# A gated state-space and attention mix: rotation tables grown from a base made on GpSimd, value sums dealt per period, the last exps cut by rows

## The chip, the cores and the metric

One core of one Trainium2 chip. The metric is the device time of one execution in microseconds (us). The kernel before took 921.59 us (median of 3 runs, 921.59 to 921.75). Below, "the span" is the time of the profiled execution from its first to its last instruction; it is 1.7 to 1.8 us shorter than the device time. PE is TensorE (PEld its weight loads), ACT is ScalarE, DVE is VectorE, POOL is GpSimd, SP is SyncE.

## The reference, cut to what matters

One sequence of 2048 positions with 1024 channels; the output is a gated mix of a diagonal state-space model and of 32-head attention.

```python
def reference(A_x, A_Lambda_re, ..., B_wqkv, B_wo, gate_w):
    x = A_x
    g = _sigmoid((x * gate_w).sum(-1, keepdims=True))
    # A: 1024 complex states
    Lam_bar = jnp.exp(dt * Lam)
    for t in range(L):
        h = Lam_bar[None, :] * h + Bu[:, t, :]        # Bu = x @ B_bar^T
    y = 2.0 * einsum("blp,dp->bld", hseq, Cmat).real + x * Dskip
    # B: 32 heads of 32 channels, no mask
    p = _softmax(scores * (Dh ** -0.5))                # [32, 2048, 2048]
    b = (p @ v) @ wo
    return g * a + (1 - g) * b
```

The softmax needs 32 x 2048 x 2048 exponentials, and they are most of the work of ScalarE.

## The kernel before

The attention runs as 512 "bursts" (the kernel's periods). Each makes scores for 4 heads, 256 queries and 256 keys in PSUM, takes two exps of 128x1024 from them and later multiplies the results with the values. In the bursts of a fixed list, half of the first exp is made on VectorE, in four instructions:

```python
def exp(self, B, z, s):
    ...
    if z == 0 and B in DVB:                 # DVB: the list of shared bursts, 96 of 512
        self.dve_exp(B, s, p)
    else:
        self.act(lambda e: e.activation(self.tile[p], ps[:, 2 * s:2 * s + 2, :], ACT.Exp, ...), ...)

def dve_exp(self, B, s, p):
    ...
    self.S.op("act", ...)                   # a half exp, 128x512, on ScalarE
    self.S.op("dve", ... tensor_scalar(xi, ps[:, 2 * s + 1, :], ...), name="exp_a")
    self.dx += [(0.603, ... "exp_b"), (0.603, ... "exp_c"), (0.603, ... "exp_d"), ...]
```

All other work fills the gaps: projections, the scan of the state-space part (by rotation tables `Et`, 512 steps for each block of 128 states), and the output projection. A small scheduler in Python puts each engine's instructions into a fixed order before the program is built; each engine then runs its own in that order.

The rotation tables are products of a fine and a coarse table, one block of states after the other:

```python
def table_ops(self, j):
    ...
    for k, y in ((0, lo), (2, lor)):
        ops.append((1.136, ... e.tensor_tensor(prod[:, k:k + 2], hi, y, ALU.mult) ...))
    for r, op in ((0, ALU.subtract), (1, ALU.add)):
        ops.append((0.6, ... e.tensor_tensor(out, prod[:, 2 * r], prod[:, 2 * r + 1], op) ...))
```

The end, after the last burst: value sums, normalization, transpose, output projection on top of preloaded sums, evacuation, two stores; and a check of the softmax's denominators whose flag every engine reads and branches on (the other path, a slower method, is never taken here):

```python
def tail(self):
    ...
    self.pv([(NBURST - 2, q) for q in range(4)])     # value sums of burst 510
    preload()
    self.pv([(NBURST - 1, q) for q in range(4)])     # value sums of burst 511
    dve(... reciprocal ...)
    for t in range(2):
        dve(... norm ...); S.op("pe", ... "xp")      # normalize, transpose
    ...                                              # check, projection, evacuation
    self.st_out(14 + r, fb)                          # two stores of 256 KB

def stream(name, e):
    S.emit(name, e, sems, MARK_AT[name], ...)        # a hint for the branch, some way ahead of it
    e.wait_ge(sems[fast.flag_op.lane], fast.flag_op.tick)
    e.reg_load(r, flag[0:1, 0:1])
    br = e.br_cmp(r, 0, on_true="done_" + name, on_false="bad_" + name, comp_op="IS_EQ")
```

## Time and profile before

| part of the profiled span | us | how read |
|---|---|---|
| start to the first exp | 9.82 | timeline of ScalarE |
| first exp to the end of the last exp | 901.70 | 9.82 to 911.52 |
| end of the last exp to the end of the last evacuation | 3.80 | to 915.32 |
| from there to the end of the span | 4.99 | to 920.31 |

The lines that carry the first two terms are in the prediction. Timeline of TensorE in the kernel before; columns: start, length, engine, line, operation, out<-in, count, and in brackets how long the engine was idle before and what released it:

```profile
909.26 1.17 PE L1765 MATMUL f_ps<-f_V,f_pt 128*128 128x33 bf16 x32
910.28 1.02 PE L2051 MATMUL f_ps<-f_Et,f_ident 128*128 128x512 bf16 x4
911.14 0.80 PE L1765 MATMUL f_ps<-f_V,f_pt 128*128 128x33 bf16 x16
912.64 0.50 PE L2066 MATMUL f_ps<-f_ident,f_On 128*128 128x128 bf16 x2 [0.70 <-DVE f_On L2063]
```

TensorE works on through the last exps: value sums of the burst before, the preload (four matmuls in 1.02 us), value sums of the last burst, and then one wait of 0.70 us for the normalization.

### The profile page before, as it was taken

How to read it: one execution, taken by the hardware profiler on the slowest of the kernel's cores; microseconds unless marked ns; L12 is line 12 of the kernel's file. 1: busy time of each engine (PE TensorE's matmuls, PEld its weight loads, DVE VectorE, ACT ScalarE, POOL GpSimd, SP SyncE). 2: the span in 40 equal slices, each digit the busy share in tenths (PEclk: the TensorE clock that was granted, in tenths of full speed). 3: DMA queues.
4: the chain of work that ended last, by engine and by line, in shares of the span. 5: the costliest groups of instructions: out<-in, count | busy, mean ns of one | idle time of the engine just before them, and what ended most of it. 6: DMA issues, size and time to landing. Idle time of an engine off the chain costs nothing.

```text
span 920.3 us, 33392 instructions
## 1 busy us (share of the span) xinstructions
PE 884.9 (96%) x14969; PEld 516.3 (56%) x15188; DVE 758.0 (82%) x1369; ACT 904.4 (98%) x1034; POOL 6.5 (1%) x31
## 2 busy tenths in 40 slices
PE   8999999999999999999999999999999999999996
PEld 4556655755575555565557555556655655555553
DVE  2799999999989889999889975669999866675665
ACT  6999999999999999999999999999999999999996
POOL 0000000000000000000000000000000000000000
PEclk9999999999999999999999999999999999999998
DMA  9546822213302324112142113123320212524312
GB/s 200 111 82 114 120 48 40 47 42 73 82 9 56 62 59 93 47 36 53 51 82 43 42 46 86 44 63 53 51 64 8 68 60 82 162 78 131 113 63 75
DMA packets 166436, 65.35 MB, mean 71 GB/s; under 512 B 146704, under 2 KB 154896, under 8 KB 166288
## 3 DMA queue, kind: packets, MB, share of 16 engines
q1 hardware_dynamic: 164128, 62.62, 30.6%
q8 instruction: 120, 1.97, 0.9%
q10 hardware_dynamic: 2160, 0.53, 0.3%
q14 instruction: 28, 0.23, 0.1%
HBM read 21.24 MB, written 12.58 MB: 37 GB/s over the span
## 4 chain that ended last, share of the span: by engine, by line
ACT 69%; PE 25%; DVE 2%; SPq 1%; issue 1%; DMA 1%; DVEq 0%
ACT f_pt L1693 59%; PE f_ps L1765 7%; PE f_ps L1677 5%; PE f_ps L1513 4%; PE f_ps L1485 4%; PE f_ps L1453 3%; ACT f_wb L1716 2%; ACT f_OT L1693 2%; ACT f_Et L1693 2%; ACT f_cT_re L1693 2%; ACT f_cT_im L1693 2%; PE f_ps L1473 1%; ACT f_ub L1716 1%; SPq L1080 1%; DMA f_xT<-in_A_x_dram 1%
## 5 line engine op out<-in xcount | busy, mean ns | idle before, releaser
L1693 ACT ACTIVATE f_pt<-f_ps 128x1024 bf16<-128x1024 f32 x848 | 801.8, 1141 | 1.2 <-PE f_ps L1677 1.0
L1765 PEld LDWEIGHTS f_ps<-f_V,f_pt 128*128 128x128 bf16 x6784 | 235.0, 96 | 136.5 <-issue 86.6
L1765 PE MATMUL f_ps<-f_V,f_pt 128*128 128x33 bf16 x6784 | 288.4, 178 | 0.3
L1677 PE MATMUL f_ps<-f_Q,f_K 32*128 32x256 bf16 x4096 | 217.9, 273 | 6.8 <-ACT f_cT_re L1693 1.0
L1677 PEld LDWEIGHTS f_ps<-f_Q,f_K 32*128 32x128 bf16 x4096 | 70.3, 92 | 122.6 <-ACT f_pt L1693 62.3
L1485 PE MATMUL f_ps<-f_xT,f_wb 128*128 128x512 bf16 x449 | 117.5, 377 | 7.2 <-issue 2.4
L1453 PE MATMUL f_ps<-f_xT,f_wb 128*128 128x512 bf16 x406 | 106.6, 378 | 5.0 <-issue 1.0
L1399 DVE TENSOR_TENSOR_SCAN f_ht<-f_pf,f_init,f_ut 128x512 bf16<-128x512 f32 x64 | 81.0, 1274 | 0.0
L1717 DVE TENSOR_SCALAR f_wb<-f_ps 128x512 f32<-128x512 f32 x77 | 52.8, 686 | 27.7 <-PE f_ps L1677 27.2
L1513 PE MATMUL f_ps<-f_cT_im,f_hp 128*128 128x512 bf16 x183 | 69.1, 378 | 3.0 <-DVE f_Ag L1522 0.5
L1540 PE MATMUL f_ps<-f_wb,f_OT 128*128 128x512 bf16 x219 | 58.0, 378 | 2.1 <-DVE f_xT L1546 0.2
L1473 PE MATMUL f_ps<-f_wb,f_xT 128*128 128x128 bf16 x896 | 59.1, 219 | 0.0
L1485 PEld LDWEIGHTS f_ps<-f_xT,f_wb 128*128 128x128 bf16 x512 | 40.2, 96 | 33.4 <-issue 1.2
L1513 PE MATMUL f_ps<-f_cT_re,f_hp 128*128 128x512 bf16 x153 | 57.8, 378 | 0.6
L1716 ACT ACTIVATE f_wb<-f_ps 128x512 bf16<-128x512 f32 x77 | 53.8, 699 | 0.0
L1724 DVE SCALAR_TENSOR_TENSOR f_wb<-f_Ag,f_wb 128x512 int16<-128x512 f32 x77 | 52.7, 684 | 0.7
L1723 DVE SCALAR_TENSOR_TENSOR f_Ag<-f_wb,f_Ag 128x512 f32<-128x512 uint16 x77 | 52.7, 685 | 0.6
L1722 DVE SCALAR_TENSOR_TENSOR f_Ag<-f_wb 128x512 f32<-128x512 uint16 x77 | 52.6, 683 | 0.1
L1453 PEld LDWEIGHTS f_ps<-f_xT,f_wb 128*128 128x128 bf16 x464 | 36.2, 96 | 28.7 <-issue 0.4
L1473 PEld LDWEIGHTS f_ps<-f_wb,f_xT 128*128 128x128 bf16 x896 | 50.5, 97 | 0.2
L1546 DVE SCALAR_TENSOR_TENSOR f_xT<-f_ps,f_gcol,f_hp 128x512 bf16<-128x512 f32 (+1 forms) x28 | 21.0, 751 | 26.6 <-PE f_ps L1540 26.6
L1391 DVE TENSOR_TENSOR f_tq<-f_ht,f_Et 128x1024 bf16<-128x1024 bf16 x64 | 42.5, 685 | 0.3
(143 smaller groups left out, 872.1 us busy)
## 6 DMA issues: line engine op xcount, KB each, us to landing
ag_scratch<-f_Ag SPq DMA_DIRECT2D x32, 256.0 KB, 2.0
f_hp<-ag_scratch SPq DMA_DIRECT2D x32, 256.0 KB, 2.8
f_wb<-in_B_wqkv_dram SPq DMA_DIRECT2D x21, 256.0 KB, 4.1
out_dram<-f_xT SPq DMA_DIRECT2D x16, 256.0 KB, 2.0
f_xa<-in_A_x_dram SPq DMA_DIRECT2D x32, 64.0 KB, 2.0
f_pf<-in_A_x_dram SPq DMA_DIRECT2D x32, 64.0 KB, 2.0
f_wb<-in_B_wo_dram SPq DMA_DIRECT2D x1, 1024.0 KB
f_OT<-f_On SPq DMA_TRANSPOSE x63, 2.3
```

The lines of the kernel that those rows point to most:

```text
L1399: ops.append((1.192, lambda ri=ri: dve(lambda e: e.tensor_tensor_scan(ht[:, ri, :], rr, ut[:, ri, :], self.init[:, ri, j:j + 1], ALU.mult, ...
L1453: mms.append((1, lambda e, f, l, a=a: e.matmul(ps[:, bank, :], w[:, g % 2, part, a, :], xT[:, a, 512 * ch:512 * (ch + 1)], start=f, stop=l ...
L1473: m = e.matmul(ps[:, bank, 128 * q:128 * (q + 1)], xT[:, a, 128 * kt:128 * (kt + 1)], w[:, g % 2, 2, a, :], start=(a == 0), stop=(a == 7))
L1485: mms.append((1, lambda e, f, l, a=a: e.matmul(ps[:, 7, :], bT[:, n % 2, ri, a, :], xT[:, a, 512 * ch:512 * (ch + 1)], start=f, stop=l), [ ...
L1513: mms.append((1, lambda e, f, l, j=j, ri=ri: e.matmul(ps[:, 7, :], hp(tq, ri, j), cT[ri][:, j, 512 * cb:512 * (cb + 1)], start=f, stop=l), ...
L1540: mms.append((1, lambda e, f, l, j=j: e.matmul(ps[:, 7, :], OT[:, j, 256 * qb + 128 * r:256 * qb + 128 * (r + 1)], wo[j][0][:, 512 * cb:51 ...
L1677: m = e.matmul(ps[:, 2 * sl[z] + h % 2, 256 * kl:256 * (kl + 1)], K[32 * h:32 * h + 32, g % 2, 128 * kt:128 * (kt + 1)], Q[32 * h:32 * h + ...
L1693: self.act(lambda e: e.activation(self.tile[p], ps[:, 2 * s:2 * s + 2, :], ACT.Exp, bias=OCTAVES * LN2, scale=LN2 / 128), [("S", s)], [("p ...
L1716: self.S.op("act", lambda e: e.activation(t[:, 0, :], ps[:, 2 * s, :], ACT.Exp, bias=OCTAVES * LN2, scale=LN2 / 128), reads=[("S", s)], wr ...
L1717: self.S.op("dve", lambda e: e.tensor_scalar(xi, ps[:, 2 * s + 1, :], BITS_0, BITS_MIN, ALU.add, ALU.max), reads=[("S", s)], writes=[("xi" ...
L1723: (0.603, lambda: self.dve(lambda e: e.scalar_tensor_tensor(xw, lo, CUBE_C, xw, ALU.add, ALU.mult), [I, W], [W], "exp_c")),
L1765: m = e.matmul(ps[:, 6, o:o + 33], self.tile[p][:, h2, 256 * kl + 128 * qt:256 * kl + 128 * (qt + 1)], V[:, g % 2, 2 * i + kl, h, :], star ...
```

## The change

Its intent: free VectorE from table work, so that more exps can be shared; fit TensorE's value sums to each period; shorten the end.

- The table's base of 128 steps is made once for all states by six operations on GpSimd; VectorE doubles it twice. The copies of the last scan column also go to GpSimd.
- The list of shared bursts grows from 96 to 101.
- The value sums are dealt per period from burst 72 on.
- The last burst's exps are cut by query halves, the tail works half by half, with four stores of 128 KB; the check moves behind the evacuations.
- GpSimd takes no part in the branch at the end.

The diff, cut to its core (`...` are cuts):

```diff
-DVB_RUNS = ((65, 65), ..., (489, 493), (498, 498), (501, 501), (508, 508))
+DVB_RUNS = ((65, 65), ..., (489, 493), (498, 498), (501, 501), (506, 510))
...
+        def products():
+            for n, (u, v) in enumerate(((0, 0), (1, 1), (0, 1), (1, 0))):
+                self.pool(lambda e, ...: e.tensor_tensor(pr[n], hi[u], lo[v], ALU.mult), ...)
+                if n % 2:
+                    self.pool(lambda e, ...: e.tensor_tensor(out, pr[n - 1], pr[n], ALU.add if r else ALU.subtract), ...)
+        ops.append((0.0, products))
...
     def table_ops(self, j):
-        for k, y in ((0, lo), (2, lor)):
-            ops.append((1.136, ... e.tensor_tensor(prod[:, k:k + 2], hi, y, ALU.mult), ...))
-        for r, op in ((0, ALU.subtract), (1, ALU.add)):
-            ops.append((0.6, ... e.tensor_tensor(out, prod[:, 2 * r], prod[:, 2 * r + 1], op), ...))
+        op(0.27, ... e.tensor_scalar(S[:, :, 0:128], bj[:, :, 0:128], w(1, 0), None, ALU.mult), ...)
+        for r, alu in ((0, ALU.subtract), (1, ALU.add)):
+            op(0.27, ... e.scalar_tensor_tensor(bj[:, r, 128:256], bj[:, r, 0:128], w(0, 0), S[:, 1 - r, 0:128], ALU.mult, alu), ...)
+        op(0.40, ... e.tensor_scalar(S, bj, w(1, 1), None, ALU.mult), ...)
+        op(0.34, ... e.tensor_copy(Et[:, :, j, 0:256], bj), ...)
+        for r, alu in ((0, ALU.subtract), (1, ALU.add)):
+            op(0.40, ... e.scalar_tensor_tensor(Et[:, r, j, 256:512], bj[:, r], w(0, 1), S[:, 1 - r], ALU.mult, alu), ...)
...
     def burst(self, B):
+        if B == NBURST - 1:                      # rows: both score buffers, 128 queries at a time
+            for t in range(2):
+                self.act(lambda e, t=t: e.activation(self.tile[...], rows[:, :, 128 * t:128 * (t + 1)], ACT.Exp, ...), ...)
+            return lambda: None
...
     def tail(self):
-        self.pv([(NBURST - 2, q) for q in range(4)])
+        self.pv([(last - 1, q) for q in range(4)])
         preload()
-        self.pv([(NBURST - 1, q) for q in range(4)])
-        dve(... reciprocal ...)
+        pv(0)
+        norm(0)
+        pv(1)
+        xp(0)
+        norm(1)
+        out(0)
+        xp(1)
+        out(1)
+        evac(0, 0, "dve")
+        evac(0, 1, "dve")
+        evac(1, 0, "act")
+        evac(1, 1, "dve")
+        for _, f in self.check(62, 64, 62, 65, 2):
+            f()
...
+            if name == "pool":
+                S.emit(name, e, sems)
+                return
             S.emit(name, e, sems, MARK_AT[name], ...)
-            if name == "pool":
-                for _ in range(272):
-                    e.nop()
```

## The prediction

> **What bounds the kernel now.** I read the page of the profile first (busy time, slices), then the chain of waits in order of time, then the timeline at both ends, then the groups of instructions by shape.
>
> The page:
>
> ```profile
> PE 884.9 (96%) x14969; PEld 516.3 (56%) x15188; DVE 758.0 (82%) x1369; ACT 904.4 (98%) x1034; POOL 6.5 (1%) x31
> ACT  6999999999999999999999999999999999999996
> ```
>
> ScalarE is full in every slice but the first and the last. PE looks nearly as full, but the groups show that its weight loads for the scores stood 62.3 us waiting for an exp to free a score buffer, so PE has room. The question is whether ScalarE's work is tight. The chain in order of time answers it:
>
> ```profile
> 145.05 19.25 ACT f_pt L1693 x21
> 164.79 54.08 ACT f_pt L1693 x59
> 904.61 0.49 ACT f_ub L1716
> ```
>
> The reader should divide: 54.08 / 59 = 0.9166 us is the pace of one full exp (128x1024), back to back; a half exp (128x512, the other half being made on VectorE) takes 0.49. The groups give the counts: 848 + 24 + 20 + 18 + 18 = 928 full and 77 + 19 = 96 half exps. At that pace they need 928 x 0.9166 + 96 x 0.49 = 850.6 + 47.0 = 897.6 us. The timeline shows when they ran (start, length):
>
> ```profile
> 9.82 1.94 ACT L1693 ACTIVATE f_pt<-f_ps 128x1024 bf16<-128x1024 f32 x2 [0.57 <-PE f_ps L1677]
> ...
> 904.97 6.55 ACT L1693 ACTIVATE f_pt<-f_ps 128x1024 bf16<-128x1024 f32 x7
> 910.93 0.47 PEld L1765 LDWEIGHTS f_ps<-f_V,f_pt 128*128 128x128 bf16 x8
> ...
> 914.05 1.27 DVE L2091 SCALAR_TENSOR_TENSOR f_xT<-f_ps,f_Et 128x512 bf16<-128x512 f32 x2
> 914.81 0.92 SPq L1571 DMA_DIRECT2D out_dram<-f_xT  x2
> ```
>
> From 9.82 to 911.52 are 901.7 us, so in 900 us ScalarE lost only about 4.1 us to waits. The span of 920.3 is therefore: 9.8 before the first exp, 897.6 of exps, 4.1 of waits, and 8.8 after the last exp (3.8 until the last evacuation ends at 915.32, the last store issued by 915.73, the rest its landing and the closing wait). Only those four terms can be changed.
>
> **What the Trainium skill says.** "ScalarE: Activation LUTs", section "What ACT_TABLE_LOAD costs", gives one element per cycle and lane at 1.2 GHz, 0.833 ns per element, for every function. The trace agrees: 0.9166 - 0.49 = 0.427 us for 512 elements, 0.833 ns each. A full exp can't get cheaper; only its work can be moved.
>
> "GPSIMD Engine Reference", section "3.1 Elementwise — side-by-side cycle accounting", gives 4497 ns for a two-input fp32 operation of 2048 elements. This trace has GpSimd only on tiny tiles (128x8 at 0.2 to 0.3 us), so it can't confirm it. My estimate from that figure: 2.25 us for 1024 elements.
>
> "SBUF — State Buffer", section "Who interferes with whom", says that a GpSimd operation that reads SBUF and a VectorE operation with two SBUF inputs, or in a 2-port mode, exclude each other for a whole instruction. No run here shows it yet; the changed kernel may.
>
> "VectorE: DVE Perf Modes", section "The perf-mode tier table (the rule you actually need)", says that each operation is capped at the mode it has a program for, single-source ones higher than two-source ones. The trace agrees:
>
> ```profile
> L1289 DVE SCALAR_TENSOR_TENSOR f_OT<-f_OT 128x400 f32<-128x400 f32 x1 | 0.6, 568 | 0.0
> L1290 DVE TENSOR_SCALAR f_OT<-f_OT 128x400 f32<-128x400 f32 x1 | 0.4, 369 | 0.0
> L1296 DVE TENSOR_SCALAR f_W<-f_W 128x16 f32<-128x16 f32 x1 | 0.2, 175 | 0.0
> L1294 DVE SCALAR_TENSOR_TENSOR f_W<-f_OT 128x16 f32<-128x16 f32 x1 | 0.2, 175 | 0.0
> ```
>
> With the 16-element forms this makes (369 - 175) / 384 = 0.51 ns per element for the one-input fp32 form and (568 - 175) / 384 = 1.02 ns for the two-input form, on 0.16 to 0.17 us fixed.
>
> **The change part by part.**
>
> (1) More half exps. The diff doesn't say so in words, but the list of bursts whose exp is shared grows from 96 to 101 (29 added, 24 removed; the count by groups of 64 bursts is +3 in the second, +1 in the seventh and eighth). ScalarE saves 5 x 0.427 = 2.1 us. VectorE gains 5 x 4 instructions of 0.685 (rows below) = 13.7 us.
>
> ```profile
> L1717 DVE TENSOR_SCALAR f_wb<-f_ps 128x512 f32<-128x512 f32 x77 | 52.8, 686 | 27.7 <-PE f_ps L1677 27.2
> L1370 DVE TENSOR_TENSOR f_OT<-f_OT 128x1024 f32<-128x1024 f32 x16 | 19.0, 1215 | 0.0
> L1374 DVE TENSOR_TENSOR f_Et<-f_OT 128x512 bf16<-128x512 f32 x16 | 11.0, 685 | 0.1
> ```
>
> (2) What pays for it on VectorE. The old rotation tables go: 16 x 1.215 + 16 x 0.685 = 30.4 us. The new ones cost per block of states one tensor_scalar of 256 (0.30), two two-input operations of 128 (2 x 0.29), a tensor_scalar of 512 and a copy of 512 (2 x 0.43), two two-input operations of 256 (2 x 0.42): 2.6 us, 20.6 for eight. The sine and cosine series shrinks from 400 to 224 columns: 15 two-input operations save 0.18 each and 7 one-input ones 0.09, together 3.3. The 24 copies of the last scan column (0.16 each, 3.8) go to GpSimd. Freed: 9.8 + 3.3 + 3.8 = 16.9, against 13.7 added, so VectorE ends near 755 us, no fuller than now. None of this is on the path by itself; it makes room for (1).
>
> (3) The base on GpSimd: four products and two sums of 1024 elements, by my estimate 6 x 2.25 = 13.5 us, where before it was busy 6.5 us in all. The order of instructions shows that the last input is made just after the seventh key evacuation, which in the trace of before ran at 25.2; so the base begins near 26.7 and ends near 40.3. The first VectorE instruction that waits for it follows the gate's reciprocal, at 40.1 to 40.5 in the trace of before. Between lie only evacuations from PSUM, which don't use the shared port. Eight table instructions (2.6 us) follow, and then the first evacuation of u, at 43.3 before. So the base is just in time; any delay beyond half a microsecond would push that evacuation, and PE with it.
>
> (4) Value sums dealt per period. A full period lasts 2 x 0.917 = 1.83 us on ScalarE and a shared one 1.41; PE's load per period is now matched to that instead of a fixed 5 or 3 quarters. This can only take from the 4.1 us of waits, of which about 0.9 lie in the opening and 1.0 before burst 72, where nothing is dealt anew. I take 0.9 of the remaining 2.2 as saved, a guess at under half, since the five new shared periods are themselves short ones that PE has to keep up with.
>
> (5) The end. The last two exps are cut by query halves, so the sums, the normalization and the transpose of the first half run under the last exp. Estimate from the last exp's end: sums 0.6, reciprocal and normalization 0.55, transpose and copy 0.6, projection 0.6, evacuation 0.7, with the first half's pieces queued in front on PE and VectorE: about 3.6 instead of 3.8. The final stores are four of 128 KB instead of two of 256, the first ones earlier, so the last has less data in front of it. The last landing took 4.1 us (915.7 to 919.8), while the median store took 2.0; I take 0.7 off. Sum for the end: 0.9. The check moves behind the evacuations; with 0.9 for its instructions and 1.0 for reading the flag (0.74 on SyncE before) it ends under the landing.
>
> (6) GpSimd out of the end branch: it was idle there and finished at 917.7, before the last store landed. Nothing. The three-fold matmuls of the rest are 8 more, at 1.02 / 4 = 0.26 at most, 2 us of PE in periods where PE waits. Nothing.
>
> Sum: 921.6 - 2.1 - 0.9 - 0.9 = 917.7 us.
>
> **The rivals.** First, the base comes late. For it: an untested GpSimd rate, the exact fit in (3), and VectorE issuing in order, so that evacuations queue behind the wait. If the six operations took twice the estimate, VectorE would stand 13 us and ScalarE perhaps 8 of them: 925 us or more. Against it: the placement looks deliberate, and the chain of before shows ScalarE not even losing 1 us there. I give a loss over 1 us one chance in six.
>
> Second, the room on VectorE isn't where it is needed. From 40 to 150 us it was busy 101.5 of 110 us, and from 150 to 300 141.1 of 150; three of the added shared exps fall just there. If evacuations came late, waits would grow by what the exps saved: 920 to 922 us. Against it: the freed table work lies in the same stretch.
>
> Third, a better end and a better fit: if the last landing took the usual 2 us, the end would give 2 instead of 0.9, and if the dealing removed 2 of the waits, the total would be 915.5. Much below that there is nothing: 9.8 + 895.5 of exps + 7 + 1.3 (measured time over span) is 913.6 with no wait at all.
>
> **Range and chances.** The sure part is 2.1; the two guesses are 0.9 each with an error near 1; the first rival lengthens the upper side. So 917.7, with 915.6 to 920.4 for eight in ten. Two per cent faster would be 903.2, which ScalarE's 895.5 us of exps alone exclude (9.8 and about 7 come on top). Two per cent slower is 940: only a broken schedule. Faster 0.01, same 0.98, slower 0.01.
>
> **What would show it.** 923 full and 101 half exps at 0.917 and 0.49; ScalarE's first exp to its last about 898.7 us; GpSimd near 25 us busy with six instructions near 2.2 us ending before 41; VectorE near 755; the last exp's end to the end of the span about 7.9 us. I am wrong if the full exp's pace changes, if VectorE waits for GpSimd over 1 us near 40, if waits inside the exps exceed 5 us, or if the end takes as long as before.

## More of the kernel before

The busy times in stretches; columns: stretch, its length, busy time (and count) of PE, PEld, DVE, ACT, POOL, then the granted clock of TensorE, the DMA share and GB/s:

```profile
909.00:912.00 3.00, 2.80 (x62) 1.92 (x57) 2.11 (x9) 2.52 (x3) 0.00 (x0) 1.00 0.19 72
```

The clock is at 1.00 here.

## The result and the profile after

The changed kernel took 925.45 us (median of 4 runs, 924.98 to 926.12), the kernel before 921.67 on the same chip. The ratio is 1.004, with a 95% interval of 1.0023 to 1.0058: the same within 2%, but slower by 3.8 us where 3.9 us less were forecast. (A ratio here is the mean time of one kernel's fast runs over the mean of the other's in the same rounds, so not quite the ratio of the medians.)

The same four terms of the span:

| part of the profiled span | before | after | forecast change | measured change |
|---|---|---|---|---|
| start to the first exp | 9.82 | 9.55 | 0 | -0.27 |
| first exp to the end of the last exp | 901.70 | 899.04 | -3.0 | -2.66 |
| last exp to the end of the last evacuation | 3.80 | 8.85 | -0.2 | +5.05 |
| last evacuation to the end of the span | 4.99 | 5.79 | -0.7 | +0.80 |
| span | 920.31 | 923.23 | -3.9 | +2.92 |

The second term came out nearly as forecast, and the end did not. (The first is no gain: in the fourteen traces the first exp starts at 9.55 to 10.16.) The page of the changed kernel:

```profile
PE 905.0 (98%) x15196; PEld 514.1 (56%) x15196; DVE 756.5 (82%) x1391; ACT 901.4 (98%) x1033; POOL 31.0 (3%) x63
PEclk9999999999999999999999999999999999999997
```

ScalarE has 3.0 us less to do (904.4 before), VectorE is no fuller than it was. (The trace of before lacks some 220 matmul records, so its lower PE figure is no change.) Was GpSimd in time with the base? Timeline of GpSimd, and the first instruction of VectorE that uses the base:

```profile
26.03 3.82 POOL L1319 TENSOR_TENSOR f_hp<-f_rc 128x1024 f32<-128x1024 f32 x2 [23.12 <-DVE f_rc L1310]
29.93 2.37 POOL L1323 TENSOR_TENSOR f_OT<-f_hp 128x1024 f32<-128x1024 f32 x1
32.24 3.83 POOL L1319 TENSOR_TENSOR f_hp<-f_rc 128x1024 f32<-128x1024 f32 x2
36.15 2.36 POOL L1323 TENSOR_TENSOR f_OT<-f_hp 128x1024 f32<-128x1024 f32 x1
```

```profile
39.92 0.35 DVE L1400 TENSOR_SCALAR f_Ag<-f_OT,f_rc 128x256 f32<-128x256 f32 x1
```

The base ends at 38.51; its first user starts at 39.92, straight behind the instruction before it, with no wait in brackets. GpSimd was busy 31.0 us, though, where the prediction expected near 25: its 24 copies of 128x2 took 12.7 us instead of 3.8. They show what the prediction left open, the exclusion of GpSimd and VectorE. Six copies took 0.19 us, five of them beside a VectorE operation that reads PSUM, one beside none. The other 18 began beside a VectorE operation with two SBUF inputs, and each ended 0.05 us after that operation did: 0.57 us (eight, beside the shared exp's steps) or 0.71 us (ten, beside a product of the scan). No engine waited visibly for this.

Now the end. Timelines of ScalarE (its last two exps) and of VectorE:

```profile
906.65 1.94 ACT L1766 ACTIVATE f_pt<-f_ps 128x1024 bf16<-128x1024 f32 x2
```

```profile
904.50 0.75 DVE L1584 SCALAR_TENSOR_TENSOR f_xT<-f_ps,f_gcol,f_xT 128x512 bf16<-128x512 f32 x1 [0.92 <-PE f_ps L1574]
905.17 0.68 DVE L1805 TENSOR_SCALAR f_ut<-f_ps 128x512 f32<-128x512 f32 x1
906.28 0.75 DVE L1584 SCALAR_TENSOR_TENSOR f_xT<-f_ps,f_gcol,f_xT 128x512 bf16<-128x512 f32 x1 [0.43 <-PE f_ps L1574]
906.95 0.68 DVE L1810 SCALAR_TENSOR_TENSOR f_ut<-f_ut 128x512 f32<-128x512 uint16 x1
907.95 0.75 DVE L1584 SCALAR_TENSOR_TENSOR f_xT<-f_ps,f_gcol,f_xT 128x512 bf16<-128x512 f32 x1 [0.32 <-PE f_ps L1574]
908.62 0.68 DVE L1811 SCALAR_TENSOR_TENSOR f_ut<-f_ut 128x512 f32<-128x512 uint16 x1
909.33 0.69 DVE L1812 SCALAR_TENSOR_TENSOR f_ub<-f_ut 128x512 int16<-128x512 f32 x1
```

The four steps of burst 510's half exp (lines 1805, 1810, 1811, 1812) start at 905.17 and end at 910.02, because two evacuations of the output projection (line 1584) stand between them in VectorE's order, each after a wait for TensorE. ScalarE had ended its last exp at 908.59. What TensorE did meanwhile:

```profile
907.96 0.25 PE L1853 MATMUL f_ps<-f_V,f_ub 128*128 128x33 bf16 x4
910.08 0.29 PE L1853 MATMUL f_ps<-f_V,f_ub 128*128 128x33 bf16 x4 [1.88 <-DVE f_ub L1812]
910.22 0.39 PE L1853 MATMUL f_ps<-f_V,f_pt 128*128 128x33 bf16 x8
910.45 1.87 PE L2162 MATMUL f_ps<-f_Et,f_ident 128*128 128x512 bf16 x4
912.11 0.43 PE L2173 MATMUL f_ps<-f_V,f_pt 128*128 128x33 bf16 x8
913.30 0.39 PE L2173 MATMUL f_ps<-f_V,f_pt 128*128 128x33 bf16 x8 [0.76 <-DVE f_On L2181]
```

It stood 1.88 us for that half exp, so the value sums of the last burst's first half began 3.52 us after the last exp, not under it. The preload took 1.87 us, where the same four matmuls took 1.02 before. And the second half's value sums waited 0.76 us for the first half's normalization, since both halves lie in one PSUM bank and the schedule keeps them apart. The stretches show why the matmuls were slow:

```profile
909.00:912.00 3.00, 1.92 (x16) 0.93 (x17) 0.99 (x2) 0.00 (x0) 0.00 (x0) 0.67 0.23 87
912.00:915.00 3.00, 1.87 (x21) 0.94 (x19) 1.27 (x7) 0.28 (x1) 0.00 (x0) 0.50 0.00 0
```

The granted clock (third number from the end) is down to 0.50. The trace has the moment: the clock record changes from 1.0 to 0.5 at 910.05. In the kernel before it did so at 915.16, when TensorE had nothing more to do.

The Trainium skill says of this, in "TensorE: Matmul & The Clock Gate", section "Part 1: The HAM clock gate (the "warmup" mystery)", that the clock is halved or full by TensorE's activity in free-running windows of 3413 ns. The traces agree on the length: the full-clock stretches last 904.53, 907.95 or 911.36 us in twelve of the fourteen traces, which are 265, 266 and 267 times 3.413.

The last term isn't in these views, which leave out branches and drains. From the trace's records: the end of VectorE's branch, the start of the drain that follows it (an instruction near the end of each engine's program), and the end of SyncE's drain:

```
                VectorE branch ends   VectorE drain starts   SyncE done   span ends
before                915.19                915.73             920.1        920.31
after                 919.68                922.95             920.1        923.23
```

Before, SyncE waited for the last store of 256 KB, whose issue began at 915.39 and which had landed by 919.83. After, the issue of the last one, of 128 KB, began at 917.47, and it had landed by 919.19, in 1.72 us instead of 4.44; but VectorE stood 3.27 us between its branch and its drain, where it stood 0.54 before. (The size is not shown to be the reason for the quicker landing. Of the sixteen parts of the old last store, twelve had landed by 917.47, 2.1 us after the issue; the last four came at 918.33 to 919.81, while instruction packets were on the queues 8 and 14 and single packets of the store took up to 0.72 us instead of 0.08. That the one held up the other is argued. In the changed kernel the engines branch only as the store lands.)

### The profile page after: what moved, and what is told of

It reads as the page before. It is cut to its first block, busy times and chain, and to the rows that moved or that the text cites. A ratio compares the mean times of both kernels' runs of the same rounds, so it can differ in the third digit from the quotient of the medians.

```text
span 923.2 us, 33694 instructions
## 1 busy us (share of the span) xinstructions
PE 905.0 (98%) x15196; PEld 514.1 (56%) x15196; DVE 756.5 (82%) x1391; ACT 901.4 (98%) x1033; POOL 31.0 (3%) x63
## 4 chain that ended last, share of the span: by engine, by line
PE 92%; ACT 3%; DVE 3%; DMA 1%; issue 0%; SPq 0%; DVEq 0%
PE f_ps L1853 26%; PE f_ps L1758 18%; PE f_ps L1517 12%; PE f_ps L1545 12%; PE f_ps L1485 11%; PE f_ps L1578 6%; PE f_ps L1505 6%; ACT f_cT_re L1781 1%; ACT f_pt L1781 1%; ACT f_cT_im L1781 1%; ACT f_OT L1781 1%; ACT f_Et L1781 1%; DMA f_xT<-in_A_x_dram 1%; DMA ag_scratch<-f_Ag 0%; DVE f_ub L1523 0%
## 5 line engine op out<-in xcount | busy, mean ns | idle before, releaser
L1758 PE MATMUL f_ps<-f_Q,f_K 32*128 32x256 bf16 x4096 | 212.9, 273 | 2.6 <-ACT f_cT_re L1781 1.0
L1758 PEld LDWEIGHTS f_ps<-f_Q,f_K 32*128 32x128 bf16 x4096 | 67.5, 92 | 121.5 <-ACT f_pt L1781 66.9
L1517 PE MATMUL f_ps<-f_xT,f_wb 128*128 128x512 bf16 x512 | 131.0, 377 | 1.0 <-DVE f_Q L1490 0.2
L1485 PE MATMUL f_ps<-f_xT,f_wb 128*128 128x512 bf16 x464 | 119.1, 378 | 0.9 <-DVE f_Ag L1554 0.2
L1805 DVE TENSOR_SCALAR f_wb<-f_ps 128x512 f32<-128x512 f32 x81 | 55.6, 686 | 33.0 <-PE f_ps L1758 31.9
L1545 PE MATMUL f_ps<-f_cT_re,f_hp 128*128 128x512 bf16 x192 | 72.6, 378 | 0.3 <-DVE f_Ag L1554 0.3
L1545 PE MATMUL f_ps<-f_cT_im,f_hp 128*128 128x512 bf16 x192 | 72.5, 378 | 0.0
L1578 PE MATMUL f_ps<-f_wb,f_OT 128*128 128x512 bf16 x248 | 64.0, 378 | 0.2
L1804 ACT ACTIVATE f_wb<-f_ps 128x512 bf16<-128x512 f32 x81 | 59.3, 733 | 0.0
L1811 DVE SCALAR_TENSOR_TENSOR f_Ag<-f_wb,f_Ag 128x512 f32<-128x512 uint16 x81 | 55.4, 684 | 0.5
L1523 DVE CAST f_ub<-f_ps 128x512 bf16<-128x512 f32 x48 | 33.1, 689 | 14.8 <-PE f_ps L1517 14.1
```

The costliest lines, as they stand in the source:

```text
L1485: mms.append((1, lambda e, f, l, a=a: e.matmul(ps[:, bank, :], w[:, g % 2, part, a, :], xT[:, a, 512 * ch:512 * (ch + 1)], start=f, stop=l ...
L1517: mms.append((1, lambda e, f, l, a=a: e.matmul(ps[:, 7, :], bT[:, n % 2, ri, a, :], xT[:, a, 512 * ch:512 * (ch + 1)], start=f, stop=l), [ ...
L1545: mms.append((1, lambda e, f, l, j=j, ri=ri: e.matmul(ps[:, 7, :], hp(tq, ri, j), cT[ri][:, j, 512 * cb:512 * (cb + 1)], start=f, stop=l), ...
L1578: mms.append((1, lambda e, f, l, j=j: e.matmul(ps[:, 7, :], OT[:, j, 256 * qb + 128 * r:256 * qb + 128 * (r + 1)], wo[j][0][:, 512 * cb:51 ...
L1758: m = e.matmul(ps[:, 2 * sl[z] + h % 2, 256 * kl:256 * (kl + 1)], K[32 * h:32 * h + 32, g % 2, 128 * kt:128 * (kt + 1)], Q[32 * h:32 * h + ...
L1804: self.S.op("act", lambda e: e.activation(t[:, 0, :], ps[:, 2 * s, :], ACT.Exp, bias=OCTAVES * LN2, scale=LN2 / 128), reads=[("S", s)], wr ...
```

## The experiments

Twelve kernels in three calls of four; each call on its own chip, with the kernel before in the same rounds (medians 922.14, 922.41 and 921.76 us). All gave correct results.

### e1_hint: the hint nearer to the branch

```diff
-    MARK_AT = dict(pe=100, act=260, dve=260, sp=900)
+    MARK_AT = dict(pe=100, act=260, dve=190, sp=900)
```

> The changed kernel with VectorE's branch hint issued 190 operations before the end instead of 260; nothing else moves. Theory A (VectorE misses the code of its branch target: its closing drain came 3.3 us after its branch, 922.95 against 919.68, while the other engines needed 0.1 to 0.5 us): the gap falls below 0.6 us, the span ends near 920.3 as SyncE's drain at 920.08 does, time about 922.5 (from 925.45). Theory B (the gap is the cost of leaving GpSimd out, or of the last stores): the gap and the time stay within 0.5 us of the changed kernel. A third outcome, that the hint is not seen at either place, looks like B.

Measured: 924.57 us (924.13 to 926.65), ratio 1.0025. VectorE's gap was 3.20 us. The hint now stood 250 of VectorE's instructions ahead of the branch instead of 334, and nothing came of it: the cure that I expected failed. (The profiled execution was the slowest of the five; ScalarE was idle for 2.1 us between 550 and 600 us. Its end is read here, not its length: from the last exp to the last evacuation 8.03 us, with the clock falling 2.64 us after the last exp, where the changed kernel's trace has 8.85 and 1.46.)

### e2_no510: no shared exp in burst 510

```diff
-(498, 498), (501, 501), (506, 510))
+(498, 498), (501, 501), (506, 506))
```

> The changed kernel with burst 510 taken out of the shared exps (100 instead of 101); only instructions of the end differ. Theory A (burst 510's VectorE half is ready only at 910.0 because three evacuations of 0.75 us stand between its four steps; PE waits 1.9 us for it, idles, its granted clock falls to 0.5 and every later matmul takes twice as long): the last exp ends 0.43 us later (near 909.0), the wait of 1.9 us is gone, the clock stays at 1.0 until about 914, preload matmuls take 1.0 us instead of 1.87, last exp to last evacuation falls from 8.85 us to 4 or 5; time near 921.3 if VectorE's late drain stays. Theory B (the clock falls because PE was 98% busy for 900 us, not because it idled): the clock is again 0.5 after 909, last exp to last evacuation stays above 6 us, time 923.5 to 924.5.

Measured: 918.92 us (918.77 to 919.12), ratio 0.9964 (0.9950 to 0.9977), by the ratios 7 us better than the changed kernel (1.004 - 0.9964 = 0.0076 of 922). TensorE and its stretch in this run:

```profile
908.77 0.76 PE L1853 MATMUL f_ps<-f_V,f_pt 128*128 128x33 bf16 x24
909.38 1.02 PE L2162 MATMUL f_ps<-f_Et,f_ident 128*128 128x512 bf16 x4
```

```profile
909.00:912.00 3.00, 2.02 (x43) 1.32 (x38) 1.48 (x6) 1.03 (x2) 0.00 (x0) 1.00 0.23 87
```

The wait of 1.88 us is gone, the clock holds, the preload takes 1.02 us again. From the last exp to the last evacuation: 4.67 us instead of 8.85. This alone is 4.2 us of the 5.05. (The evacuations between the four steps were two, not three as I had written.) Two things I hadn't foreseen: VectorE's gap fell to 0.53 us by itself, and 4.67 is still 0.87 more than the 3.80 of before.

### e4_both: hint and no shared exp in 510

Both diffs above.

> Both edits together. If the two are independent, their gains add: about 921.3 - 3.0 = 918.3 us, and the kernel is faster than the one before by some 3 us, near the 917.7 of the prediction. If one edit merely uncovers the other (the end is a maximum of both), the gain is that of the larger one alone, 921 to 922.

Measured: 918.54 us (917.99 to 918.71), ratio 0.9959; last exp to last evacuation again 4.67, gap 0.53. It adds nothing to e2 but a repetition, since the gap was gone already; that the time came near the 918.3 of adding gains is luck, as the hint gave none.

### e5_prefirst: the preload ahead of the wait

```diff
-        self.pv([(last - 1, q) for q in range(4)])
         preload()
+        self.pv([(last - 1, q) for q in range(4)])
```

> The changed kernel with burst 510 kept shared, but the four preload matmuls put ahead of its value sums, so that PE works through the first 0.9 us of the wait. Theory A: the idle time shrinks from 1.9 to about 1.0 us; the preload leaves the path (1.87 us at half clock); if the clock then holds, last exp to last evacuation falls from 8.85 to about 5.5 us and the time to about 922; if a pause of 1 us already lowers the clock, to about 7, time near 923.6. Theory B for the clock: it is 0.5 whatever the pause, time near 923.6.

Measured: 923.32 us (922.80 to 923.71), ratio 1.001. Last exp to last evacuation 7.0 us. With the shared exp kept and the preload put into its wait, TensorE's longest pause was 1.01 us, and the clock still fell, at 912.46. So the late half exp costs in two ways, by the wait and by the clock, and filling the wait pays only for a part.

### e6_pad24: VectorE's branch moved by 24 places

Six kernels had by now shown the gap or not: before, with the branch at place 1503 of VectorE's instructions (accumulator reads left out), and e2 and e4 at 1526 had none; after, e1 and e5 at 1530 had it. That points to the place. So I moved the branch and nothing else:

```diff
+        pad = es.enter_context(nc.sbuf_tensor("pad", [1, 32], F32))
...
+            if name == "dve":
+                for k in range(24):
+                    e.memset(pad[:, k:k + 1], 0.0)
             S.emit(name, e, sems, MARK_AT[name], ...)
```

> The changed kernel with 24 tiny memsets (one element each, to a scratch that nobody reads) at the start of VectorE's program; nothing else. They stand before VectorE's first work, where it waits for loads anyway, and move its branch at the end by 24 instructions. Theory A (the 3.3 us between VectorE's branch and its closing drain are a fetch of the branch's target, and whether it is hidden depends on where in the instruction stream the branch stands: the kernels with the branch at place 1503 and 1526 had no gap, those at 1530 had it): the gap falls from 3.3 to about 0.5 us, SyncE's drain ends the span, and the time falls by 2.5 to 3.1 us, to 922.3 to 923.0, about the kernel before. Theory B (the gap comes of how VectorE is loaded at the end, not of the place): gap stays 3.2 us, time 925.4. Theory C (memsets at the start cost): time above 925.4.

Measured: 922.30 us (921.72 to 923.83), ratio 1.0006 (0.9992 to 1.0020), where the changed kernel had 1.0040: 24 needless instructions save 3.1 us. The gap was 0.52 us. The views of the DMA queues show a difference too. From 902 to 912 us the changed kernel has one packet of instructions, this one two (queue and kind; packets, MB, share). First the changed kernel, then this one:

```profile
q8 instruction: 1, 0.02, 0.8%
```

```profile
q8 instruction: 1, 0.02, 0.6%
q14 instruction: 1, 0.01, 0.5%
```

The packet on queue 14, at 906.81 us, is VectorE fetching its next piece of program, 25 instructions ahead of its branch. (Which engine a packet of queue 14 is for is inferred: those put down to VectorE follow one another at 123 to 132 of its records, and shift with the memsets.)

One point of caution: the clock fell in this run at 912.86, not at 910.05, which made the way to the last evacuation 7.92 instead of 8.85 us. About 0.9 us of this profiled run's gain is that. The trace is of use for it: the value sums of the last burst begin 2.67 us after the last exp, with the clock still full up to there, where they begin at 3.52 in the changed kernel and at 0.40 in e2.

### e7_no510_pad4: the gap brought back

The version of e2 with 4 such memsets, which put its branch back to place 1530.

> The version without the VectorE half in burst 510 (918.9 us, no gap, branch at place 1526) with 4 such memsets, which put VectorE's branch back to place 1530, that of the changed kernel. Theory A (place): the gap of about 3.2 us returns and the time rises by 2.4 to 3.1 us, to 921.3 to 922.0. Theory B (load at the end): no gap, 918.9. The end up to the last evacuation stays 4.7 us after the last exp in either case.

Measured: 922.03 us (921.42 to 923.89), ratio 0.9998, where e2 had 0.9964: 3.1 us lost to four memsets of one element. The gap was 3.50 us and ended the span; last exp to last evacuation stayed at 4.66. With e6 this settles it: the place of the branch makes the gap, not the load of VectorE and not the hint. The table, with VectorE's last fetch ahead of the branch counted in its records:

| kernel | last fetch ahead of the branch | gap, us |
|---|---|---|
| before | 99 | 0.54 |
| after, e1, e5 | 129 | 3.27, 3.20, 3.25 |
| e7 | 131 | 3.50 |
| e2, e4 | 125 | 0.53, 0.53 |
| e6 | 25 | 0.52 |
| e8 (both), e12 | 22 | 0.52, 0.52, 0.52 |
| e9, e10 | 26 | 0.52, 0.52 |
| e11 | 124 | 0.52 |

With a fetch about every 128 instructions, the next one falls just on the branch in the kernels of the second and third row, and 3 to 29 records behind it, or well ahead of it, in the others. (In e11 the branch stands at place 1527, three before that of the changed kernel, and has no gap.) The Trainium skill, "Runtime: NRT & Kernel Launch", section "Instruction fetch mechanics", says that a taken branch whose target isn't among the two pages held forces a fetch before execution goes on. The trace agrees as far as it goes: in the four kernels with the gap, four packets go over queue 14 at the end, three of them while VectorE stands and one after its drain has begun; the other versions of the changed kernel have three in all. Which page was thrown out for which isn't in the records; that part is argued.

### e8_order and e8_again: the preload in the wait for the normalization

The obvious remedy for the wait of 0.76 us is to let the second half's value sums go on while the first half is normalized. It can't be tried in this layout: both halves are in one PSUM bank, and the program that checks a kernel before it may run refuses a write there while VectorE reads it. But TensorE can do something else in that time:

```diff
-        preload()
         pv(0)
         norm(0)
+        preload()
         pv(1)
```

without the shared exp in 510, and with the 24 memsets.

> Candidate for the best version: no VectorE half in burst 510, 24 memsets (branch away from the place of the gap), and at the end the order value sums of the first half, their normalisation, preload of the last sums, value sums of the second half, so that TensorE does the preload while it has to wait for the normalisation. Theory A (the wait of 0.76 us for the normalisation is on the path): last evacuation ends 3.9 to 4.1 us after the last exp, where 4.67 was measured, and the time is 917.9 to 918.3. Theory B (the preload lay in a wait already, or what follows it is bound by VectorE): 4.6 us and 918.5 to 918.9.

Measured: 919.42 us (917.98 to 920.80), ratio 0.9969 (0.9956 to 0.9983). Last exp to last evacuation was 3.81 us, as expected; but the time lies above the 917.9 to 918.3 that I expected: ScalarE was idle for 1.4 us in the stretch from 550 to 600, where e2 was for 0.4 (VectorE and with it TensorE stood behind a transfer to the scratch memory). The traces of e7 and e1 show the same, 1.6 and 2.1 us, and that of the second run of this very kernel 0.2, so it is a chance of the run:

> The best candidate a second time, byte for byte (no VectorE half in burst 510, 24 memsets, preload behind the first normalisation), on another chip or day, to settle its size: if it beats the kernel before by what the traces add up to (2.9 us from the exps, and an end of 3.8 + 2.9 us where the kernel before has 3.8 + 5.0), its time is 917.5 to 919.5 and the ratio 0.996 to 0.997.

Measured: 917.80 us (917.73 to 919.45), ratio 0.9961 (0.9948 to 0.9975). Timeline of TensorE:

```profile
908.86 0.35 PE L2173 MATMUL f_ps<-f_V,f_pt 128*128 128x33 bf16 x8
909.28 0.81 PE L2162 MATMUL f_ps<-f_Et,f_ident 128*128 128x512 bf16 x3
909.98 0.35 PE L2173 MATMUL f_ps<-f_V,f_pt 128*128 128x33 bf16 x8
```

No wait in brackets is left: value sums, preload (one record of its four is missing), value sums. It is the best version that I ran, 3.6 to 4.0 us ahead of the kernel before (by ratio and by medians) and, by the ratios, 7.3 ahead of the changed one.

### e12_noorder: the same with the old order

> The same without the moved preload: the old order at the end. Theory A (the 0.76 us for which TensorE waits for the first normalisation are on the path of the end): last exp to last evacuation 4.67 us where the moved preload has 3.81, and 0.7 to 0.9 us more time than e8_again in the means. Theory B (the gain in the trace was chance): no difference.

Measured: 918.56 us (918.36 to 919.07), ratio 0.9966; last exp to last evacuation 4.67 us against 3.81. In the medians the new order is worth 0.76 us, in the means 0.5, because one run of e8_again was at 919.45. The gain in the trace is certain, in the times it is at the edge of the spread.

### e9_basedve: the base back on VectorE, in one piece

On the version of e8:

```diff
-                self.pool(lambda e, n=n, u=u, v=v: e.tensor_tensor(pr[n], hi[u], lo[v], ALU.mult), ...)
+                self.dve(lambda e, n=n, u=u, v=v: e.tensor_tensor(pr[n], hi[u], lo[v], ALU.mult), ...)
...
-                    self.pool(lambda e, ...: e.tensor_tensor(out, pr[n - 1], pr[n], ...), ...)
+                    self.dve(lambda e, ...: e.tensor_tensor(out, pr[n - 1], pr[n], ...), ...)
```

> The same as e8_order with the six products and sums of the table's base back on VectorE instead of GpSimd (this part of the change undone alone). By the trace of the changed kernel VectorE is idle for 18 per cent of the span, but in the opening it makes the tables before it can help. My reading (VectorE has room, and the base on GpSimd bought little by itself; 6 operations of about 1.1 us each on VectorE): +0 to +1.0 us against e8_order, part of it as exps waiting in 23 to 45 us. Rival (the opening is tight on VectorE: GpSimd's base carries the gain): +3 us or more.

Measured: 926.51 us (926.22 to 927.24), 7.2 us over e8_order in the means. I had expected at most 1.0: wrong, and the rival right. Timelines of VectorE, TensorE and ScalarE:

```profile
26.87 2.35 DVE L1319 TENSOR_TENSOR f_hp<-f_rc 128x1024 f32<-128x1024 f32 x2
29.25 1.23 DVE L1323 TENSOR_TENSOR f_OT<-f_hp 128x1024 f32<-128x1024 f32 x1
32.78 1.22 DVE L1323 TENSOR_TENSOR f_OT<-f_hp 128x1024 f32<-128x1024 f32 x1
33.92 0.42 DVE L1188 CAST f_K<-f_ps 128x256 bf16<-128x256 f32 x1
```

```profile
34.40 0.61 PE L1758 MATMUL f_ps<-f_Q,f_K 32*128 32x256 bf16 x8 [6.63 <-DVE f_K L1188]
```

```profile
35.05 1.02 ACT L1781 ACTIVATE f_cT_re<-f_ps 128x1024 bf16<-128x1024 f32 x1 [6.23 <-PE f_ps L1758]
```

The six operations hold VectorE from 26.87 to 34.0; the evacuation of keys queues behind them, TensorE's next scores wait for the keys, and ScalarE waits 6.23 us for the scores. (TensorE's clock was at 0.5 from 31.30 to 38.13 in this run, and from 29.85 to 33.26 in e10; what that adds isn't parted from the rest.) Idle time on an engine elsewhere is no room here.

### e10_basespread: the same, dealt between the evacuations

The six operations entered singly, at 1.17 us each, so that the scheduler spreads them.

> The base of the table on VectorE again, but its six operations entered singly with their measured cost of 1.17 us, so that the scheduler deals them between the evictions instead of putting all six in one piece of 7.1 us ahead of the key and value evictions as in e9_basedve (which cost 7.3 us, in one wait of 6.3 us at 36 us). Theory A (what cost 7.3 us was the single piece; dealt out, VectorE's idle time of some 7 to 8 us between 26 and 40 us takes most): +0.3 to +2.5 us against e8_again. Theory B (VectorE has no room in the opening whatever the order): +5 us or more.

Measured: 920.94 us (920.72 to 921.41), ratio 0.9990, 2.8 us over e8_again in the means. It falls between the two theories, a little above the first: dealing them out saves more than half of the loss, yet exps still wait 1.2 us near 30 and again near 33. So GpSimd's base is worth about 3 us against the best that I tried on VectorE, more than the 0 to 1 that I gave it.

### e11_fewhalves: five shared exps fewer

The version of e8 without the shared exps of bursts 446, 462, 465, 470 and 473 (a choice that the scheduler accepts).

> The same as e8_again with five of the VectorE halves taken away (bursts 446, 462, 465, 470, 473), so ScalarE does five full exps more in their place. It tests the term of the prediction that says 0.427 us for each half (0.9166 less 0.49). If the exps are the bound there: +2.1 us (1.8 to 2.4) against e8_again. If waits take the place of the halves: less than 1 us.

Measured: 919.88 us (919.65 to 920.76), ratio 0.9981: +1.9 us in the means, +2.1 in the medians, and ScalarE's first exp to its last took 901.51 us against 899.59. The term of the prediction, 2.1 us for five halves, holds.

## Why the prediction was wrong

**What held.** (1) Five more halves: forecast -2.1; e11 gives 1.9 to 2.1 for five. (2) VectorE near 755: 756.5. (3) The base: 12.4 us on GpSimd (forecast 13.5), ending at 38.5, without a wait. The first rival fell by these lines, and e9 and e10 show what stood behind it. (4) By the prediction's own sum the waits within the exps are 899.04 - 923 x 0.9166 - 101 x 0.49 = 3.5 us, so 0.6 less than 4.1 where 0.9 less was guessed; no run parts this from the rest. Together, first exp to last 899.04 where about 898.7 was forecast.

Three readings of the prediction were loose without changing its outcome. The 4.1 us are a remainder: idle time of ScalarE between its exps is only 0.9 us of them in the trace (0.5 after), the rest is in the spacing of exps that follow each other. The last landing's 4.1 us count from the end of the issue and the median's 2.0 from its start; from the start it is 4.4. And the measured time is 1.8 us over the span of the profiled run (922.11 against 920.3), not 1.3. (A block's table also takes seven instructions, as its (2) lists, not eight.)

**The step that failed: (5), the end.** The prediction took 0.9 off, "about 3.6 instead of 3.8" to the last evacuation and 0.7 for the landing. Measured: 8.85 and 5.79. Its terms were added up for the tail alone, at the rates of before, with the first half's work "under the last exp", where it began only 3.52 us after it. What was missing:

- *The late half exp.* The new list ends on burst 510, whose value sums stand ahead of the preload. I counted the list's members and didn't ask what its last member does to the end: its four steps alternate with evacuations on VectorE and end 1.4 us after ScalarE's last exp.
- *The clock.* With the pause of 1.88 us, TensorE's clock was halved from 910.05 on, for nearly all matmuls of the tail. With the two together gone, e2 has 4.67 instead of 8.85: 4.2 us, most of the miss. My estimate of how they divide is from three traces. Up to the last burst's value sums e2 needs 0.40 us, e6, with the half exp but still the full clock, 2.67, and the changed kernel 3.52; from there on e2 needs 4.27 us, e6 and the changed kernel, at half clock for most or all of it, 5.26 and 5.33. So the late half exp alone is 2.3 us, and the clock 0.85 + 1.06 = 1.9 us.
- *The wait for the first normalization.* "The first half's pieces queued in front" didn't see that the second half's sums wait for VectorE: 0.76 us in the trace, 0.86 in e12 against e8_again. With all three repaired the end takes 3.81 us, that of before: the new tail as a whole bought nothing in any run, and 3.6 was too hopeful. The cut by rows alone was not tested.
- *The branch.* In (6) I wrote "Nothing" of the end branch and looked at GpSimd only. The last store did take 2.7 us less to land than the old one, more than the 0.7 that I took, though not shown to be for its size. But VectorE's branch had come to a place where it costs 3 us more: e6 and e7 take this away and bring it back by moving the branch alone. Without it, the closing is 2.85 us in e8_again, 2.1 less than before.

So the gain of 2.7 us within the exps was real and was given back at the end: 5.05 before the last evacuation, 0.80 after it. The range missed this since all three rivals looked at the opening, the room on VectorE and a better end; none had an end that gets worse.

## What to carry to other kernels

When a list, a ratio or a placement is tuned, look at its last members: work that is free in the middle of a kernel stands bare at the end, where nothing covers a late helper. Let TensorE run without pauses up to its last matmul, and fill a wait that can't be removed with work that was due anyway. Where the end of a kernel with a branch loses some 3 us that no timeline shows, compare the records of branches and drains, and move the branch by a few instructions to see.

## What the Trainium skill lacked or had wrong

- "TensorE: Matmul & The Clock Gate", section "HAM oscillation — how this bites in real kernels", gives as the rule that there be no idle gaps over about 3.4 us. The page also tells of short idles that bring the clock down in another kernel, but it gives no share of a window. Here the clock fell after pauses of 1.88 us (after) and of 1.01 us with shorter ones (e5). In all fourteen traces, the full clock ended with the first window of 3.413 us in which TensorE was busy with matmuls, as the profile models them, for 0.51 of the time or less (0.40 after, 0.47 in e5, 0.49 in e12, 0.51 before), and went on through windows with 0.56 and more (0.56 in e8_order, 0.57 in e2). It is busy share in a window that fits these runs, not the length of a gap, and the phase of the window decides a part: the same tail lost its clock 1.46 us after the last exp in the trace of the changed kernel, 2.64 us after it in e1 and 3.67 us after it in e6.
- "Runtime: NRT & Kernel Launch", section "Instruction fetch mechanics", speaks of blocks of 16 KiB, 256 instructions. Queue 8, which by its 120 packets for some 30,400 instructions is TensorE's, does carry packets of 16 KiB; but queue 14 carries 8 KiB, and VectorE's fetches come about every 128 instructions. The page doesn't say what a branch costs that stands just where such a fetch is due: 3.2 to 3.5 us from branch to drain instead of 0.52 to 0.54, at both distances of the hint that were tried (334 and 250 instructions, e1).
- "GPSIMD Engine Reference", section "3.1 Elementwise — side-by-side cycle accounting": its 4497 ns for 2048 elements scales to 2.25 us for 1024. The sums took 2.36, the products with broadcast inputs 1.94; on VectorE the same took 1.2 (e9). That is near the figure. No page that I read has the copy of 128x2 that moved to GpSimd: 0.19 us there alone, 0.57 or 0.71 beside a VectorE operation with two SBUF inputs, against 0.16 on VectorE.
